# Packed scores on 64 by 32 tiles of TensorE, without the block-diagonal operand, and another order of the first element pairs

## The chip, the core and the metric

The kernel runs on one core of a Trainium2 chip. The metric is device time in microseconds (us), from launch to the last byte of the output. Engines in the text: PE is TensorE, PEld its weight loads, DVE is VectorE, ACT is ScalarE, POOL is GpSimd, SP is SyncE, which issues nearly all the DMAs here.

## What is computed

Three stages, one after the other. The first is attention through 32 packed queries per head, the only one that the change touches:

```python
s = scale * matmul(p, k^T);  a = softmax(s);  p_packed = matmul(a, v)      # 32 x 576 scores for each head
s = scale * matmul(q, p_packed^T);  out = matmul(softmax(s), p_packed)     # 576 x 32 scores for each head
```

There are 4 batch elements, 8 heads, 576 positions and 64 numbers per head. The second stage is a mixture of four experts (2304 tokens, 512 to 1024 to 512), the third one a layer `g = h - tanh(h)` with 2048 hidden columns. Everything is float32.

## The kernel before

**What a packed score costs.** Two heads lie on the 128 partitions of one k tile (`kv_k[b][j]`, head r on partitions 64r to 64r+63), so four k tiles j make one batch element b. They are taken in two groups g of two tiles (four heads). `pack_mm(b, g)` (L253) computes the scores of a group: for each tile two products of 288 columns with `pbd`, an operand of 128 rows by 64 columns that holds the two heads' queries on its diagonal blocks and zeros elsewhere, so that one product over 128 rows gives both heads' scores apart. `pbd` is made from the loaded queries `pst` by `proto` (L1062): a DVE copy for the upper and an ACT copy for the lower half, in three pieces (four tiles at the start, the tokens `D04` and `D48` for the rest), after two memsets on POOL. float32 products appear in the trace as two records each.

**What follows a group.** `pack_max` (DVE: a maximum over 576 columns, L267, and a scaling, L269), `pack_exp` (ACT, L276, with the row sums), `pack_norm` (DVE, L284 to L287), `pack_T` (PE transposes L301 and L302, ACT copies L306 and L307), `pack_pv` (PE products with v, L319, copies L326 on ACT and L327 on DVE into `ppbd`). Then for each pair of token tiles `q_mm` and `q_max` (L341, L354), `q_exp` (L365 DVE, L368 ACT), `q_sum` and `q_mul` (L374 to L383 on DVE), `q_T` (PE L398, ACT L401, DVE L402, into `a2h` and `a2l`). The scores of a group live in a PSUM tile of the pool `ps2`, which has two buffers; the products `wps` of `pack_w1` (L584) and the projections `hps` of `up` (L634) use the same two.

**What sets the order.** Strings of tokens written by hand. `START_A`, `START_L`, `START_B` cover the first 75 us; `FIRST` and others follow. A token is a stage letter with its indices (table `STAGES`): in `M10`, M is `pack_mm`, 1 the pair of elements and 0 the group counted over the pair (M10 and M11 are the third element's two groups, M12 and M13 the fourth's). A is `pack_max`, c `pack_exp`, E both, N `pack_norm`, T `pack_T`, P `pack_pv`, Q and O `q_mm` (a whole tile pair, or half of the j), J `q_exp`, R `q_sum` with `q_mul`, X `q_T`, W `pack_w1`, u and U `up` (the second projection onto the experts' hidden columns), d, h and j `down` (L739, products of 512 columns), b `prep` (ACT copy L553 of a w2 block), B `low_w2` (its rest on DVE, L545), K, V, L loads, D `proto`. PE, DVE, ACT and SP keep the written order in `START_A` and `START_L`; PE keeps it to the end, SP in the strings after. An engine works through its own row in that order: an instruction that waits holds back all that stand behind it on its engine.

Of the kernel before, what the change touches and what calls it, by code (L numbers as in the profile page):

```python
# [9 lines left out]
F32 = mybir.dt.float32  # L10
F32R = mybir.dt.float32r
U32 = mybir.dt.uint32
ACTF = mybir.ActivationFunctionType
# [42 lines left out]
MIN_HI_SQ = (1.125 * 2.0 ** -15) ** 2  # L56

START_A = (
    "f9 f1 M00 E00 M01 E01 N00 N01 f5 T00 T01 P00 P01 D04 Q00 J00 Q01 R00 W000 f6 X00 M02 K2 b00 E02 D48 B0 N02 "
)  # L60

START_L = (
    "u000 b01 J01 T02 M03 B1 E03 n N03 d000 P02 T03 R01 M10 P03 A10 X01 c10 Q02 J02 K3 V2 V3 Q03 R02 W001 O040 O041 "
    "M11 h001 X02 j001 A11 G04 c11 J03 J04 r03 I1 U0010 t03 U0011 R04 N10 "
)

START_B = (
    "a010 a011 d002 X03 X04 M12 A12 T10 c12 N11 N12 u002 M13 A13 T11 c13 N13 P10 d003 C00 T12 P11 u003 T13 W100 P12 W101 "
    "d004 P13 "
    "L2 a110 a111 k00 k01 C01 "  # L70
)
# [48 lines left out]
def kernel(  # L120
# [13 lines left out]
    nc = tc.nc  # L134
    B, S_LEN = v.shape[0], v.shape[1]
# [5 lines left out]
    def pool(name, bufs=1, stack=None, **kw):  # L141
        return (stack or ctx).enter_context(
            tc.tile_pool(name=name, bufs=bufs, **kw, **({} if kw.get('space') == DRAM else {'reuse_waits': 'tile'}))
        )
# [9 lines left out]
    p_w1 = pool("w1", 2, pa)  # L154
    p_k4 = pool("k4", 5, pa)
    p_pp = pool("pp", 2, pa)
    pbd = p_k4.tile([128, 4 * B, 64], F32, tag="k", name="pbd")
    pps = ExitStack()
    ps2 = pool("ps2", 2, pps, space=PSUM)
    ps1 = pool("ps1", 2, pps, space=PSUM)  # L160
# [5 lines left out]
    def p1t(shape, name):  # L166
        n = (4 if warm_done else 3) if psx else 1
        turn[0] += 1
        pl = psx[0] if psx and turn[0] % n > 1 else ps1
        return pl.tile(shape, F32, tag="p1" if pl is ps1 else "x1", name=name)  # L170
    p_w2 = pool("w2", 8, pa)
    att_stack = ExitStack()
    p_att = pool("att", 8, att_stack)
# [29 lines left out]
    def att_tile(b, shape, name):  # L203
        if b < 1:
            return p_att.tile(shape, F32, tag="a", name=name)
        return u2t(shape, F32, name)

    kv_k, kv_v, qs = {}, {}, {}
# [41 lines left out]

    scs, nms = {}, {}

    def pack_mm(b, g):  # L253
        sc = scs[b, g] = ps2.tile([128, 2, 512], F32, tag="p2", name="sc")
        for jj in range(2):
            j = 2 * g + jj
            for h in range(2):
                nc.tensor.matmul(  # L258
                    out=sc[64 * jj:64 * jj + 64, h, 0:288],
                    lhsT=pbd[:, 4 * b + j, :],  # L260
                    rhs=kv_k[b][j][:, 288 * h:288 * h + 288],
                )

    def pack_max(b, g):
        sc = scs[b, g]
        mx = small.tile([128, 1], F32, tag="mx", name="mx")
        nc.vector.tensor_reduce(out=mx, in_=sc[:, :, 0:288], op=ALU.max, axis=AX.XY)  # L267
        nm = small.tile([128, 1], F32, tag="nm", name="nm")
        nc.vector.tensor_scalar(out=nm, in0=mx, scalar1=-0.125, scalar2=None, op0=ALU.mult)  # L269
        nms[b, g] = nm  # L270

    def pack_exp(b, g):
        sc, nm = scs.pop((b, g)), nms.pop((b, g))
        a1 = att_tile(b, [128, S_LEN], "a1")
        ss = small.tile([128, 1], F32, tag="ss", name="ss")
        nc.scalar.activation(  # L276
            out=a1.rearrange("p (h s) -> p h s", h=2), in_=sc[:, :, 0:288],
            func=ACTF.Exp, scale=0.125, bias=nm, accum_out=ss,
        )
        a1s[b, g] = a1, ss  # L280
# [9 lines left out]
    def pack_scores(b, g):  # L290
        pack_mm(b, g)
        pack_max(b, g)
        pack_exp(b, g)
        pack_norm(b, g)
# [15 lines left out]
    def pack_pv(b, g):  # L310
        a1t, a1e = a1ts.pop((b, g))
        bi = b % 2
        pv = p1t([128, 2, 32], "pv")
        for jj in range(2):
            j = 2 * g + jj
            for c in range(5):
                for h in range(2):
                    k0 = 64 * jj + 32 * h
                    nc.tensor.matmul(  # L319
                        out=pv[64 * h:64 * h + 64, jj, :],  # L320
                        lhsT=kv_v[b][c][:, 128 * j + 64 * h:128 * j + 64 * h + 64],
                        rhs=a1t[:, c, k0:k0 + 32] if c < 4 else a1e[:, k0:k0 + 32],
                        start=(c == 0), stop=(c == 4),
                    )
        js = slice(2 * g, 2 * g + 2)
        nc.scalar.activation(out=ppbd[b // 2][0:64, bi, js, 0:32], in_=pv[0:64], func=ACTF.Copy)  # L326
        nc.vector.tensor_copy(out=ppbd[b // 2][64:128, bi, js, 32:64], in_=pv[64:128])  # L327
# [33 lines left out]
    def q_exp(p, t0):  # L361
        n, G, sc3, mx = a2s[p, t0]
        a2 = u2t([128, 512], F32, "a2")
        a23 = a2[:, 0:n].rearrange("p (g k) -> p g k", k=32)
        nc.vector.tensor_tensor(  # L365
            out=a23, in0=sc3, in1=mx[:, 0:G].to_broadcast([128, G, 32]), op=ALU.subtract
        )
        nc.scalar.activation(out=a2[:, 0:n], in_=a2[:, 0:n], func=ACTF.Exp, scale=0.125)  # L368
        a2s[p, t0] = a2, a23, G
# [36 lines left out]
    def pp_init(p):  # L406
        ppbd[p] = p_pp.tile([128, 2, 4, 64], F32, tag="ppbd", name="ppbd")
        nc.gpsimd.memset(ppbd[p], 0.0)
# [577 lines left out]
    def late_norm():  # L986
# [3 lines left out]
    STAGES = {  # L990
        "S": lambda p, i: pack_scores(2 * p + i // 2, i % 2),
        "M": lambda p, i: pack_mm(2 * p + i // 2, i % 2),
        "E": lambda p, i: (pack_max(2 * p + i // 2, i % 2), pack_exp(2 * p + i // 2, i % 2)),
        "A": lambda p, i: pack_max(2 * p + i // 2, i % 2),
        "c": lambda p, i: pack_exp(2 * p + i // 2, i % 2),
# [3 lines left out]
        "t": lambda p, i: q_mul(p, 2 * i),  # L999
        "T": lambda p, i: pack_T(2 * p + i // 2, i % 2),  # L1000
        "P": lambda p, i: pack_pv(2 * p + i // 2, i % 2),
        "Z": pp_split,
        "I": pp_init,
# [9 lines left out]
        "a": stage,  # L1013
        "b": prep,
        "B": low_w2,
        "D": lambda a, n: proto(slice(4 + a, 4 + a + n)),
        "J": lambda p, i: q_exp(p, 2 * i),
        "k": save_w2,
        "W": pack_w1,
# [20 lines left out]
    blank = u2t([128, 128], F32, "blank")  # L1040
    nc.vector.memset(blank, 0.0)
    warm = psx[0].tile([128, 4, 128], F32, tag="x1", name="warm")
    pst = p_att.tile([128, 4 * B, 32], F32, tag="a", name="pst")
    with tc.manual_schedule(engines={mybir.EngineType.SP}):
        nc.scalar.dma_start(out=pst[:, 0:4], in_=pT[:, 0:4])
        load_k(0)
# [12 lines left out]
    for i, val in enumerate((P2, Q, -T2, 0.0)):  # L1059
        nc.vector.memset(cst[:, i:i + 1], val)  # L1060
    nc.scalar.activation(out=cst[:, 3:4], in_=cst[:, 0:1], func=ACTF.Exp)
    def proto(j):  # L1062
        nc.vector.tensor_copy(out=pbd[0:64, j, 0:32], in_=pst[0:64, j])
        nc.scalar.activation(out=pbd[64:128, j, 32:64], in_=pst[64:128, j], func=ACTF.Copy)

    nc.gpsimd.memset(pbd[:, 0:4], 0.0)
    proto(slice(0, 4))
    make_identity(nc, ident)
    nc.gpsimd.memset(pbd[:, 4:], 0.0)
    pp_init(0)  # L1070
    zero_tail()
    zero_tail()
# [270 lines left out]
```

## Time and profile before

| | us |
|---|---|
| median of 3 runs (1050.61 to 1051.05) | 1050.85 |
| the profiled execution, whole time | 1050.9 |
| its span from first to last instruction | 1049.1 |
| PE busy in the span | 1041.8 |
| DVE busy | 882.9 |
| ACT busy | 622.4 |

The profile of one execution says for each engine how long it was busy (a table by stretches of the span), lists instructions in order of time with what ended an idle stretch before them (the timeline: start, duration, engine, line, operation, output<-inputs, shapes, count, then in brackets the idle time and its releaser), and follows back the chain of work that ended last. That chain is PE for 97% of the span, so the question for every stretch is whether PE has work there and what it waits for.

### The profile page before, as it was taken

To read this page: it belongs to the slowest core of one execution; us is meant where nothing else is said; L and a number is where in the kernel's file an instruction comes from. 1 tells how busy PE (TensorE), PEld (TensorE's weight loads), DVE (VectorE), ACT (ScalarE), POOL (GpSimd) and SP (SyncE) were. 2 spreads that over 40 slices of the span, in tenths; PEclk is the share of its full clock that TensorE was granted. 3 is DMA by queue.
4 is the path that set the end of the run, shared out by engine and by line. 5 is a ranking of instruction groups with operands and counts; after the bars stand their busy time and mean duration, and the time that the engine had idled before them with its cause. 6 is when DMAs were issued, how large, how long until landed. Compare 5 with 4: busy or idle time off the path is not lost.

```text
span 1049.1 us, 16510 instructions
## 1 busy us (share of the span) xinstructions
PE 1041.8 (99%) x6345; PEld 897.1 (86%) x6345; DVE 882.9 (84%) x1356; ACT 622.4 (59%) x987; POOL 161.6 (15%) x134
## 2 busy tenths in 40 slices
PE   8999999999999999999999999999999999999998
PEld 6788888888888888888888888998999899899897
DVE  5878987988987776989897986789988899988877
ACT  4555555545454355454454444678877778777775
POOL 1000032312423102424242431000000000000000
PEclk9999999999999999999999999999999999999999
DMA  9766445544663355375446254354455453574442
GB/s 345 239 204 217 153 141 179 203 172 137 215 221 130 142 186 188 122 237 181 125 187 251 93 199 183 118 221 151 180 221 196 195 211 142 200 266 162 184 171 81
DMA packets 57727, 192.75 MB, mean 184 GB/s; under 512 B 6448, under 2 KB 9136, under 8 KB 54576
## 3 DMA queue, kind: packets, MB, share of 16 engines
q1 hardware_dynamic: 57360, 191.49, 50.9%
q8 instruction: 50, 0.82, 0.3%
q14 instruction: 29, 0.24, 0.1%
q10 hardware_dynamic: 288, 0.20, 0.1%
HBM read 144.74 MB, written 46.92 MB: 183 GB/s over the span
## 4 chain that ended last, share of the span: by engine, by line
PE 97%; DVE 0%; ACT 0%; issue 0%
PE yps L739 38%; PE ops L1162 19%; PE h3ps L933 17%; PE hpx L682 8%; PE hpz L682 6%; PE wps L584 3%; PE hps L634 2%; PE pv L319 1%; PE qsc L341 1%; PE sc L258 1%; PE xps L848 0%; PE qtp L398 0%; PE tp L301 0%; PE xps L808 0%; PE ops L1192 0%; DVE qsm L374 0%
## 5 line engine op out<-in xcount | busy, mean ns | idle before, releaser
L1162 PE MATMUL ops<-wo,gh 128*128 128x512 f32 x574 | 177.6, 390 | 0.0
L1162 PEld LDWEIGHTS ops<-wo,gh 128*128 128x128 f32 x574 | 107.1, 188 | 20.5
L752 DVE SCALAR_TENSOR_TENSOR x<-yps,pn,x 128x512 f32<-128x512 f32 x126 | 93.9, 746 | 30.6 <-PE yps L739 30.1
L739 PE MATMUL yps<-w2h,h0h 128*128 128x512 f32 x288 | 115.8, 402 | 0.0
L739 PE MATMUL yps<-w2h,h0l 128*128 128x512 f32 x288 | 113.4, 394 | 0.1
L739 PE MATMUL yps<-w2h,h1h 128*128 128x512 f32 x288 | 113.1, 393 | 0.0
L739 PE MATMUL yps<-w2l,h0h 128*128 128x512 f32 x288 | 112.9, 392 | 0.0
L1162 PE MATMUL ops<-wo,gl 128*128 128x512 f32 x287 | 112.6, 392 | 0.0
L739 PE MATMUL yps<-w2h,h1l 128*128 128x512 f32 x288 | 112.5, 391 | 0.0
L739 PE MATMUL yps<-w2l,h1h 128*128 128x512 f32 x288 | 112.1, 389 | 0.0
L933 PE MATMUL h3ps<-xh,wg 128*128 128x384 f32 x384 | 103.6, 336 | 0.0
L943 ACT ACTIVATE h<-h3ps 128x384 f32<-128x384 f32 x96 | 46.9, 490 | 70.6 <-PE h3ps L933 70.6
L455 POOL TENSOR_TENSOR fo<-fo,f 128x512 f32<-128x512 f32 x32 | 43.6, 1364 | 268.9 <-DVE f L451 183.3
L682 PE MATMUL hpx<-th,wp 128*128 128x288 f32 x336 | 80.7, 295 | 0.0
L739 PEld LDWEIGHTS yps<-w2h,h0h 128*128 128x128 f32 x288 | 54.0, 187 | 20.8 <-issue 11.3
L933 PEld LDWEIGHTS h3ps<-xh,wg 128*128 128x128 f32 x384 | 69.9, 188 | 0.7
L949 DVE TENSOR_TENSOR h<-h3ps,h 128x384 f32<-128x384 f32 x72 | 39.9, 554 | 30.6 <-PE h3ps L933 26.2
L739 PEld LDWEIGHTS yps<-w2h,h0l 128*128 128x128 f32 x288 | 54.0, 188 | 12.8 <-DVE h0l L619 0.6
L739 PEld LDWEIGHTS yps<-w2h,h1l 128*128 128x128 f32 x288 | 54.1, 188 | 12.3
L739 PEld LDWEIGHTS yps<-w2l,h1h 128*128 128x128 f32 x288 | 54.1, 188 | 12.1
L933 PE MATMUL h3ps<-xl,wg 128*128 128x384 f32 x192 | 64.3, 335 | 0.0
L739 PEld LDWEIGHTS yps<-w2h,h1h 128*128 128x128 f32 x288 | 54.1, 188 | 11.6
(192 smaller groups left out, 2587.3 us busy)
## 6 DMA issues: line engine op xcount, KB each, us to landing
wg<-wing SPq DMA_DIRECT2D x24, 1792.0 KB, 7.3
wraw<-in_w_dram SPq DMA_DIRECT2D x48, 512.0 KB, 6.3
wo<-wout SPq DMA_DIRECT2D x48, 512.0 KB, 8.8
w2s<-w2h SPq DMA_DIRECT2D x16, 512.0 KB, 4.1
w2s<-w2l SPq DMA_DIRECT2D x16, 512.0 KB, 3.8
f<-in_win_dram SPq DMA_DIRECT2D x16, 512.0 KB, 5.6
f<-in_wout_dram SPq DMA_DIRECT2D x16, 512.0 KB, 4.3
wing<-f SPq DMA_DIRECT2D x32, 256.0 KB, 3.7
```

Source lines behind the costliest of these rows:

```text
L258: nc.tensor.matmul(out=sc[64 * jj:64 * jj + 64, h, 0:288], lhsT=pbd[:, 4 * b + j, :], rhs=kv_k[b][j][:, 288 * h:288 * h + 288],)
L319: nc.tensor.matmul(out=pv[64 * h:64 * h + 64, jj, :], lhsT=kv_v[b][c][:, 128 * j + 64 * h:128 * j + 64 * h + 64], rhs=a1t[:, c, k0:k0 + 32 ...
L455: nc.gpsimd.tensor_tensor(out=lf, in0=lf, in1=st[:, :, 1].bitcast(F32), op=ALU.mult)
L584: nc.tensor.matmul(out=ps[32 * j:32 * j + 32, r, :], lhsT=ppbd[p][d, bi, j, 32 * r:32 * r + 32], rhs=raw[0, c, j // 2][d, j % 2, :],)
L634: nc.tensor.matmul(out=ps[:, ff, 0:n], lhsT=a[c, p, bi][:, g, c0:c0 + 128], rhs=x[p][:, g, t0:t0 + n], start=(k == 0), stop=(k == 5),)
L682: nc.tensor.matmul(out=ps[:, ff, 0:HB], lhsT=W[a][:, slot, c0], rhs=x[b], start=(start and k == 0), stop=(stop and k == 2), skip_group_che ...
L739: nc.tensor.matmul(out=ps, lhsT=a[:, ff, o:o + 128], rhs=w[c, fp][:, ff], start=(k == 0), stop=(k == 11),)
L752: last[0] = nc.vector.scalar_tensor_tensor(out=x2[tt], in0=ps, scalar=pn[:, tt, e:e + 1], in1=x2[tt], op0=ALU.mult, op1=ALU.add,).ins
L933: nc.tensor.matmul(out=ps, lhsT=wg[n][:, a, slot, 128 * kk:128 * kk + 128], rhs=x[c][b][kk] if isinstance(x[c][b], list) else x[c][b][:, k ...
L943: nc.scalar.activation(out=hs[n][a][b], in_=xz[n]["XZ".index(i)], func=ACTF.Copy)
L949: nc.vector.tensor_tensor(out=t, in0=xz[n]["XZ".index(i)], in1=t, op=ALU.add)
L1162: nc.tensor.matmul(out=ps, lhsT=a, rhs=wo[n][ff][:, w], start=(i == 0 and ff == 0 and k == 0), stop=(i == NG - 1 and ff == 1 and k == 2), ...
```

## The change

Three things change.

The scores no longer use `pbd`. A product takes 64 partitions of k (one head) and 32 columns of queries straight from `pst`, and writes 32 partitions of the score tile; `place` gives the partitions. There are twice as many products, each on a quarter of the array of 128 by 128. `pbd`, its memsets and `proto` with its tokens go.

`pack_mm` can take both groups of an element in one run (token `m`), alternating between the groups, with the places in the second group exchanged so that eight products in a row stand on eight different tiles. It is used for the third element (`m2`) and the fourth (`m3`).

The order strings change. `b00` comes after `E02`. The third element's two groups move from `M10` (ahead of `P03`) and `M11` (after `O041`) to `m2` after `R02`, with `X01` ahead of `P03`; its maxima and exponentials stand there together. `W001` moves from ahead of `O040` to the end of `START_L`. `m3` takes the place of `M12` and `M13` and stands where M12 stood.

```diff
 START_A = (
-    "f9 f1 M00 E00 M01 E01 N00 N01 f5 T00 T01 P00 P01 D04 Q00 J00 Q01 R00 W000 f6 X00 M02 K2 b00 E02 D48 B0 N02 "
+    "f9 f1 M00 E00 M01 E01 N00 N01 f5 T00 T01 P00 P01 Q00 J00 Q01 R00 W000 f6 X00 M02 K2 E02 b00 B0 N02 "
 )
 START_L = (
-    "u000 b01 J01 T02 M03 B1 E03 n N03 d000 P02 T03 R01 M10 P03 A10 X01 c10 Q02 J02 K3 V2 V3 Q03 R02 W001 O040 O041 "
-    "M11 h001 X02 j001 A11 G04 c11 J03 J04 r03 I1 U0010 t03 U0011 R04 N10 "
+    "u000 b01 J01 T02 M03 B1 E03 n N03 d000 P02 T03 R01 X01 P03 Q02 J02 K3 V2 V3 Q03 R02 m2 A10 c10 A11 c11 "
+    "O040 O041 h001 X02 j001 G04 J03 J04 r03 I1 U0010 t03 U0011 R04 N10 W001 "
 )
 START_B = (
-    "a010 a011 d002 X03 X04 M12 A12 T10 c12 N11 N12 u002 M13 A13 T11 c13 N13 P10 d003 C00 T12 P11 u003 T13 W100 P12 W101 "
+    "a010 a011 d002 X03 X04 m3 A12 c12 A13 T10 N11 c13 N12 d003 T11 N13 P10 C00 P11 u002 T12 u003 T13 W100 P12 W101 "
     "d004 P13 "
 ...
-    def pack_mm(b, g):
-        sc = scs[b, g] = ps2.tile([128, 2, 512], F32, tag="p2", name="sc")
-        for jj in range(2):
-            j = 2 * g + jj
-            for h in range(2):
-                nc.tensor.matmul(
-                    out=sc[64 * jj:64 * jj + 64, h, 0:288],
-                    lhsT=pbd[:, 4 * b + j, :],
-                    rhs=kv_k[b][j][:, 288 * h:288 * h + 288],
-                )
+    def place(b, g, jj, r):
+        return 64 * jj + 32 * (r ^ (g if b > 1 else 0))
+
+    def pack_mm(b, *gs):
+        for g in gs:
+            scs[b, g] = ps2.tile([128, 2, 512], F32, tag="p2", name="sc")
+        for h in range(2):
+            for jj in range(2):
+                for r in range(2):
+                    for g in gs:
+                        j, d = 2 * g + jj, slice(64 * r, 64 * r + 64)
+                        k0 = place(b, g, jj, r)
+                        nc.tensor.matmul(
+                            out=scs[b, g][k0:k0 + 32, h, 0:288],
+                            lhsT=pst[d, 4 * b + j, :],
+                            rhs=kv_k[b][j][d, 288 * h:288 * h + 288],
+                        )
 ...
-                    k0 = 64 * jj + 32 * h
+                    k0 = place(b, g, jj, h)
 ...
+        "m": lambda b: pack_mm(b, 0, 1),
 ...
-    def proto(j):
-        nc.vector.tensor_copy(out=pbd[0:64, j, 0:32], in_=pst[0:64, j])
-        nc.scalar.activation(out=pbd[64:128, j, 32:64], in_=pst[64:128, j], func=ACTF.Copy)
-
-    nc.gpsimd.memset(pbd[:, 0:4], 0.0)
-    proto(slice(0, 4))
     make_identity(nc, ident)
-    nc.gpsimd.memset(pbd[:, 4:], 0.0)
```

The lines of the functions named above stand seven higher in the changed kernel (L267 becomes L274). SP's row is the same in both.

On ACT, from the split of the first pair's scores (`a2h`) on, before:

```order
L401 ACTIVATE a2h_214<-qtp_399 128x2x256
L553 ACTIVATE w2h_419<-wraw_173 128x1024
L276 ACTIVATE a1_427,ss_428<-sc_406,nm_425 128x576
L1064 ACTIVATE pbd_81<-pst_137 64x8x32
L618 ACTIVATE h0h_444<-hps_448 128x2x256
```

and in the changed kernel:

```order
L408 ACTIVATE a2h_209<-qtp_400 128x2x256
L283 ACTIVATE a1_428,ss_429<-sc_407,nm_426 128x576
L560 ACTIVATE w2h_431<-wraw_172 128x1024
L625 ACTIVATE h0h_447<-hps_451 128x2x256
L625 ACTIVATE h1h_449<-hps_466 128x2x256
```

The copy of the w2 block (`w2h`) now stands behind the exponential of M02's scores. On DVE the order at this place is as before (maximum, scaling, `w2l` of B0, then the norm N02 of the same scores), less the copy into `pbd`.

On PE, from the transposes of T03 on to the first products of h001, before (P03 is the four rows `pv`, Q02 and Q03 are `qsc` x32, W001 is `wps`, O040 and O041 are `qsc` x8):

```order
L301 MATMUL tp<-ident,a_507 128x128 x4
L302 MATMUL te<-ident,a_507 64x128
L258 MATMUL sc<-kt,pbd 64x288 x4
L319 MATMUL pv<-a1t,vt 64x32 x8
L319 MATMUL pv<-a1e,vt 64x32 x2
L319 MATMUL pv<-a1t,vt 64x32 x8
L319 MATMUL pv<-a1e,vt 64x32 x2
L398 MATMUL qtp<-ident,a_482 128x128 x4
L341 MATMUL qsc<-ppbd,qt 64x2x32 x32
L584 MATMUL wps<-wraw,ppbd 32x512 x8
L341 MATMUL qsc<-ppbd,qt 64x2x32 x8
L258 MATMUL sc<-kt,pbd 64x288 x4
```

and in the changed kernel:

```order
L308 MATMUL tp<-ident,a_514 128x128 x4
L309 MATMUL te<-ident,a_514 64x128
L405 MATMUL qtp<-ident,a_485 128x128 x4
L326 MATMUL pv<-a1t,vt 64x32 x8
L326 MATMUL pv<-a1e,vt 64x32 x2
L326 MATMUL pv<-a1t,vt 64x32 x8
L326 MATMUL pv<-a1e,vt 64x32 x2
L348 MATMUL qsc<-ppbd,qt 64x2x32 x32
L265 MATMUL sc<-kt,pst 32x288 x16
L348 MATMUL qsc<-ppbd,qt 64x2x32 x8
```

X01 (`qtp`) moved from behind M10 and P03 to directly behind T03; both groups of scores stand in one run; W001 has left this place.

On DVE, from the row sums of R02 on, before:

```order
L374 TENSOR_REDUCE qsm_679<-a2_635 128x16
L375 TENSOR_SCALAR qsm_679<-qsm_679 128x16
L378 RECIPROCAL qsm_679<-qsm_679 128x16
L383 TENSOR_TENSOR a2_635<-a2_635,qsm_679 128x512
L595 TENSOR_TENSOR wp_693<-wps_684,wp_693 128x1024
L402 TENSOR_TENSOR a2l_215<-qtp_717,a2h_214 128x2x256
L267 TENSOR_REDUCE mx_732<-sc_705 128x1
L269 TENSOR_SCALAR nm_734<-mx_732 128x1
```

and in the changed kernel:

```order
L381 TENSOR_REDUCE qsm_674<-a2_630 128x16
L382 TENSOR_SCALAR qsm_674<-qsm_674 128x16
L385 RECIPROCAL qsm_674<-qsm_674 128x16
L390 TENSOR_TENSOR a2_630<-a2_630,qsm_674 128x512
L274 TENSOR_REDUCE mx_697<-sc_679 128x1
L276 TENSOR_SCALAR nm_699<-mx_697 128x1
L274 TENSOR_REDUCE mx_704<-sc_680 128x1
L276 TENSOR_SCALAR nm_706<-mx_704 128x1
L291 TENSOR_SCALAR ss_709<-ss_709 128x1
L409 TENSOR_TENSOR a2l_210<-qtp_727,a2h_209 128x2x256
```

Both maxima of the third element, with a step that waits for an exponential, now stand ahead of X02's `a2l`; on ACT both exponentials stand ahead of its `a2h`. W001's `wp` stands behind the norms N10, further on.

## Rows read from the trace of the kernel before

**Rows 1.** Busy time by stretches: length, then each engine; PEclk, DMA share, GB/s

```profile
20.00:75.00 55.00, 54.41 (x617) 42.26 (x618) 43.52 (x98) 31.48 (x65) 1.98 (x7) 1.00 0.70 234
75.00:1045.00 970.00, 970.00 (x5496) 840.83 (x5496) 829.58 (x1232) 583.24 (x907) 155.32 (x112) 1.00 0.49 177
```

**Rows 2.** Timeline, the first scores: start, duration, instruction, idle before and releaser

```profile
1.06 4.14 PE L984 MATMUL warm<-blank 128*128 128x128 f32 x20 [1.06 <-DVE cst L1060]
...
5.48 2.21 PE L258 MATMUL sc<-kt,pbd 128*64 128x288 f32 x16 [0.28 <-ACT pbd L1064]
```

**Rows 3.** Timeline, PE at M10, W001 and M11

```profile
31.70 1.20 PE L258 MATMUL sc<-kt,pbd 128*64 128x288 f32 x8
...
36.57 1.09 PE L584 MATMUL wps<-wraw,ppbd 64*32 64x512 f32 x16
...
...
38.10 1.19 PE L258 MATMUL sc<-kt,pbd 128*64 128x288 f32 x8
```

**Rows 4.** Timeline, from M02's scores to the transposes of T02

```profile
21.56 1.06 ACT L553 ACTIVATE w2h<-wraw 128x1024 fp32r<-128x1024 f32 x1 [0.94 <-DMA wraw<-in_w_dram]
...
22.04 0.15 DVE L269 TENSOR_SCALAR nm<-mx 128x1 f32<-128x1 f32 x1
...
22.52 0.72 ACT L276 ACTIVATE a<-sc,nm 128x576 f32<-128x576 f32 x1
...
22.65 1.23 DVE L545 TENSOR_TENSOR w2l<-wraw,w2h 128x1024 fp32r<-128x1024 f32 x1 [0.26 <-ACT w2h L553]
...
23.36 0.42 ACT L1064 ACTIVATE pbd<-pst 64x256 f32<-64x256 f32 x1
...
24.18 0.52 DVE L287 TENSOR_SCALAR a<-a,rs 128x576 f32<-128x576 f32 x1
...
24.93 0.60 PE L301 MATMUL tp<-ident,a 128*128 128x128 f32 x4
```

**Rows 5.** Timeline, from T02's successors to X01 and Q02

```profile
25.76 0.69 DVE L619 SCALAR_TENSOR_TENSOR h1l<-hps,h1h 128x512 fp32r<-128x512 f32 x1 [0.46 <-ACT h1h L618]
...
31.03 0.63 PE L301 MATMUL tp<-ident,a 128*128 128x128 f32 x4
...
31.55 0.69 DVE L374 TENSOR_REDUCE qsm<-a 128x16 f32<-128x512 f32 x1
...
32.72 0.61 PE L319 MATMUL pv<-a1t,vt 128*64 128x32 f32 x16
32.77 0.69 DVE L383 TENSOR_TENSOR a<-a,qsm 128x512 f32<-128x512 f32 x1
...
33.97 0.66 PE L398 MATMUL qtp<-ident,a 128*128 128x128 f32 x4
...
34.55 2.08 PE L341 MATMUL qsc<-ppbd,qt 128*64 128x64 f32 x64
```

**Rows 6.** Timeline, from R02's product to the projection U0010

```profile
39.43 0.69 DVE L383 TENSOR_TENSOR a<-a,qsm 128x512 f32<-128x512 f32 x1
...
40.04 1.22 DVE L595 TENSOR_TENSOR wp<-wps,wp 128x1024 fp32r<-128x1024 f32 x1
...
41.34 0.60 ACT L401 ACTIVATE a2h<-qtp 128x512 fp32r<-128x512 f32 x1 [2.26 <-PE qtp L398]
...
41.97 0.69 DVE L402 TENSOR_TENSOR a2l<-qtp,a2h 128x512 fp32r<-128x512 f32 x1 [0.72 <-ACT a2h L401]
...
42.58 0.75 DVE L267 TENSOR_REDUCE mx<-sc 128x1 f32<-128x576 f32 x1
...
42.72 0.19 PEld L634 LDWEIGHTS hps<-a2l,wp 128*128 128x128 f32 x1 [0.22 <-DVE a2l L402]
```

**Rows 7.** Timeline, a wait in d002, the norms N10 and N11, M12

```profile
47.06 0.19 PEld L739 LDWEIGHTS yps<-w2h,h0l 128*128 128x128 f32 x1 [0.58 <-DVE h0l L619]
...
49.87 0.95 DVE L287 TENSOR_SCALAR a<-a,rs 128x576 f32<-128x576 f32 x2
...
50.25 1.20 PE L258 MATMUL sc<-kt,pbd 128*64 128x288 f32 x8
```

More of the change, by code (lines that the diff above doesn't have):

```diff
@@ L156 @@
     p_pp = pool("pp", 2, pa)
-    pbd = p_k4.tile([128, 4 * B, 64], F32, tag="k", name="pbd")
+    pst = p_k4.tile([128, 4 * B, 32], F32, tag="k", name="pst")
     pps = ExitStack()
@@ L1015 @@
         "B": low_w2,
-        "D": lambda a, n: proto(slice(4 + a, 4 + a + n)),
         "J": lambda p, i: q_exp(p, 2 * i),
@@ L1042 @@
     warm = psx[0].tile([128, 4, 128], F32, tag="x1", name="warm")
-    pst = p_att.tile([128, 4 * B, 32], F32, tag="a", name="pst")
     with tc.manual_schedule(engines={mybir.EngineType.SP}):
```

## The prediction

> **What bounds the kernel now.** I read the busy time by stretches first, since it says where a gain or a loss would count. From 75 to 1045 us PE is busy for all of 970 us at a granted clock of 1.00, and from 20 to 75 us for 54.41 of 55 [rows 1]. So PE is the bound behind the first 20 us, and it has no idle time in which a delay could be made good: what PE is late by at 75 us, the kernel is late by at the end. The whole change lies ahead of 75 us. I then went through the timeline of that stretch, PE's row beside the rows of DVE and ACT, and asked at each moved token two things: how much PE time it saves, and whether what PE needs next is ready in the new order.
>
> The second question matters because 54.41 of 55 us busy means that nearly every hand-off in the stretch is hidden by something, and the change moves what hides it. PE also doesn't run past a product that waits: in d002 it stood 0.58 us for `h0l` [rows 7], with the following products of the same two weights standing behind it.
>
> I write how much later (+) or earlier (-) PE comes to a place than before.
>
> **The price of the new scores.** Before, a group is four products of 288 columns on two tiles of 128 by 64, two on each; M10 starts at 31.70 and P03 behind it at 32.72 [rows 3, 5], so 1.0 us, and M11 lasts about 1.1 [rows 3]. Now a group alone is eight products on four tiles, again two on each: I take the same 1.1. The only row with tiles of 64 by 32 is W001: eight products of 512 columns on eight tiles in 1.09 us [rows 3]. A run of both groups is sixteen products of 288 columns on the same eight tiles, two on each: 2 x 1.09 x 288/512 = 1.2, less what stands in both once (the tail), so 1.1. Against 2.1 for two groups apart, `m2` and `m3` save 1.0 us of PE each. The bounds: 1.0 for a run (no fixed cost twice) and 2.2 (the two row halves not beside each other, a rival below).
>
> The rest that goes, three pieces of `proto` on DVE and ACT (0.3 to 0.42 each, as the 0.42 at 23.36 [rows 4]) and two memsets on POOL, is off PE's path except at the very start. There the first scores waited 0.28 us for ACT's copy [rows 2]; the products of the first fill end at 1.06 + 4.14 = 5.20. With the copy gone PE can start there: **-0.3**, which the chain of hand-offs behind it passes on up to M02.
>
> **T02: ACT's new order.** Before, `w2h` ran first (21.56, when its DMA had landed) and M02's exponential at 22.52, behind it [rows 4]; on DVE `w2l` ran from 22.65 while the exponential went on, and the norm followed it, ending at 24.18 + 0.52 = 24.70, just before PE came to T02 at 24.93. Now the exponential goes first: the scaling ends at 22.19, less 0.3, so it starts at 22.0 and ACT is free 0.84 later (22.52 to 23.36 in rows 4), at 22.85. `w2h` takes 1.06, to 23.9. On DVE the norm still stands behind `w2l`, and from the start of `w2l` to the norm's end it was 2.05 us (22.65 to 24.70). That gives 26.0, and T02 at 26.1: **+1.2**. PE has nothing to do there for about 1.5 us, since its projection before T02 comes 0.3 to 0.6 earlier. What is queued behind on DVE (`h0l`, `h1l`, J01, B1, the maximum of M03) moves too, but there DVE had 0.46 us of idle time [rows 5], which absorbs part: I take **+0.8** at T03, so 31.8 for 31.03.
>
> **X01: its cover is gone.** R01 begins once P02's copy is through, at 31.55 before, and its last product ended at 32.77 + 0.69 = 33.46 [rows 5]. Before, M10 and P03 (31.70 to 33.97) stood on PE between T03 and X01 and hid it. Now X01 stands directly behind T03, which ends at about 32.4, while R01 ends at 33.46 + 0.8 = 34.3: PE waits 1.9 us, X01 starts at 34.35 for 33.97, **+0.4** though M10 (1.0) and P03 (1.25) are still to come. P03 then takes 1.25 and X01 0.6: Q02 at 36.1 for 34.55, **+1.5**. Q02's second half reads what P03's copies give; X01 hid that before and now doesn't: another 0.3. Then W001 has gone (1.0) and `m2` takes the place of M11 at the same price: **+0.8** where h001 begins.
>
> **U0010: two more steps on DVE and ACT ahead of X02's split.** R02's product on DVE was at 39.43 [rows 6]; with Q02 it comes 1.4 to 1.5 later and ends at 41.6. Before, `wp` (1.22) stood next, then `a2l`, which was through when PE wanted it: PE's idle at U0010's second product was 0.22 us [rows 6]. Now two maxima with their scalings stand there (0.75 and 0.15 each [rows 4, 6]), and on ACT two exponentials of 0.84 ahead of `a2h` (0.60). The first exponential starts at 41.6 + 0.95 = 42.55, the second ends at 44.25, `a2h` at 44.9, `a2l` (0.69) at 45.55; PE goes on at 45.6 for 42.72: **+2.9**. h001, X02 and j001 cover PE up to about 43.6, so it idles near 2 us here. W001, now behind U0011, adds its 1.0 again, and the wait of d002 (0.58, some 0.4 of it lost time) falls away under it: **+3.5**.
>
> **m3: the gain and a new wait.** It saves 1.0. But it takes both buffers of `ps2` at once, and the second is W001's, free only when DVE has done `wp` (1.22 [rows 6]), which now stands behind both norms. These ended at 49.87 + 0.95 = 50.8 [rows 7]; 2.8 to 3.5 later, with 1.22 behind them, gives 54.8 to 55.5, while PE comes to `m3` at 50.25 + 3.5 = 53.75. So 1.05 to 1.75 of waiting for 1.0 saved: +0.1 as I take it. What is moved behind it (T10 to P13, d003 now ahead of T11) keeps one block of 2.7 us or more on PE ahead of each thing that it needs; I count nothing, with 0.4 either way.
>
> **Sum.** +3.6 us on PE at 75 us, and so at the end. From the profiled execution's 1050.9 (the median of the runs is 1050.85): **1054.5 us**, 0.34% slower. In other words: 2.0 of PE's time and 0.3 at the start are saved, and some 6 us of new idle time on PE stand against them, at T02 (1.5), X01 with Q02 (2.2), U0010 (2.0) and `m3` (1.1), less the 0.6 or so of waits that go.
>
> **Rivals.** *PE fills the new waits.* If PE took the products that stand behind a waiting one, as long as their own operands are there, P03 would run in X01's wait and W001 or U0011 in U0010's; the new idle time would fall from 6 us to under 1, and with 2.3 saved the kernel would end at 1049.5, faster. It decides from 3.6 us of filled time on. The weight loads do run ahead of the products, which speaks for it; the 0.58 us stood in d002 speaks against it [rows 7]. 3%.
>
> *Shorter hand-offs.* The chains at T02, X01, U0010 and `m3` hold some 25 steps between engines, of 0.03 to 0.1 us each as rows 4 to 6 show them. If the changed order lets 0.06 of each overlap, 1.5 us go: 1053.0. Only beyond that would it lie within 0.2% of before (2.1 us, about what a measurement of this kernel can tell from no change). 5% for under 2.1.
>
> *The two row halves don't run side by side.* In W001 the two row halves of the array write different PSUM banks; no row shows two of them writing one bank at the same time, in different partitions, as each group now does. If that goes one after the other, each of the four single groups takes 1.0 more on the path and each of the two runs 1.0: some 6 us, 1060.5. [...] I give it 8%, since the row that is nearest, W001's, has row halves and column strips side by side at no loss.
>
> *The clock.* [...] 4%.
>
> **How the numbers follow.** My forecast, 1054.5, has 80%. Its own range comes from the terms: hand-offs 1.5 less at most, `m3` and what follows 1.0 more, the other waits 0.3 each: 1052.9 to 1056.6, which takes in the clock's case; the bank's case and those that end within 0.2% or faster, together under 20%, are left out. Slower by over 0.2% (the forecast, the bank, the clock): 92%. Within: 5%. Faster: 3%.
>
> **What would show it.** In the changed profile: the first scores at about 5.2; ahead of T02's transposes PE idle about 1.5 us and released by DVE's norm; ahead of X01 1.9 us released by R01's product; ahead of U0010 1.3 us released by ACT's `a2h` and more by `a2l`; the runs `m2` and `m3` at 1.1 us of products, `m3` with a wait for `wp` inside; PE busy for all of the time behind 80 us. I am wrong if PE comes to the fourth element's scores (50.25 before) less than 2.1 us later, or if a single group takes 2 us.

## The result, and the profile after

The changed kernel takes 1056.70 us (median of 6 runs, 1055.68 to 1057.22) against 1050.95 (1050.61 to 1051.51): a ratio of 1.0053, 95% interval 1.0043 to 1.0064, so 0.53% slower, where 0.34% was forecast. The median lies 0.1 us above the upper end of the forecast's range. The profiled execution of the changed kernel took 1055.77 us, its span is 1053.9.

Where the time is lost shows in the same two stretches as in rows 1 (columns as there):

```profile
20.00:75.00 55.00, 50.59 (x622) 39.80 (x620) 40.00 (x88) 27.64 (x59) 2.13 (x8) 0.97 0.62 208
75.00:1045.00 970.00, 970.00 (x5533) 840.51 (x5526) 830.18 (x1234) 585.11 (x909) 155.28 (x112) 1.00 0.50 178
```

(The third number from the end is the granted clock.) Between 20 and 75 us PE is busy for 50.59 us where it was 54.41, and the mean granted clock there is 0.97 for 1.00. Behind 75 us PE has no idle time in either kernel, as forecast: from W100 on each place of PE's row stands 4.83 us later than in the first trace of before, up to the end.

The timeline of the changed kernel, PE's row at the places that the prediction speaks of:

```profile
21.00 1.18 PE L265 MATMUL sc<-kt,pst 64*32 64x288 f32 x16
27.29 0.66 PE L308 MATMUL tp<-ident,a 128*128 128x128 f32 x4 [1.34 <-DVE a L294]
33.33 0.66 PE L308 MATMUL tp<-ident,a 128*128 128x128 f32 x4
35.99 0.63 PE L405 MATMUL qtp<-ident,a 128*128 128x128 f32 x4 [1.90 <-DVE a L390]
37.78 3.57 PE L348 MATMUL qsc<-ppbd,qt 128*64 128x64 f32 x64
41.28 1.20 PE L265 MATMUL sc<-kt,pst 64*32 64x288 f32 x32
43.02 0.50 PE L746 MATMUL yps<-w2h,h0h 128*128 128x512 f32 x1
47.07 0.41 PE L641 MATMUL hps<-a2h,wp 128*128 128x320 f32 x1 [0.56 <-ACT a2h L408]
47.80 0.42 PE L641 MATMUL hps<-a2l,wp 128*128 128x320 f32 x1 [0.32 <-DVE a2l L409]
55.24 0.82 PE L405 MATMUL qtp<-ident,a 128*128 128x128 f32 x6
55.98 1.97 PE L265 MATMUL sc<-kt,pst 64*32 64x288 f32 x32
71.99 1.09 PE L591 MATMUL wps<-wraw,ppbd 64*32 64x512 f32 x16
```

These are M02, T02, T03, X01, Q02 with Q03, `m2`, h001, U0010 (two rows), X03, `m3` and W100. The waits at T02 and X01 stand in brackets with the releasers that were forecast. What was not: the 64 records of Q02 and Q03 take 3.57 us for 2.08. The granted clock of that stretch says why:

```profile
36.00:37.68 1.68, 1.68 (x43) 1.51 (x44) 0.40 (x1) 0.60 (x1) 0.00 (x0) 1.00 0.83 281
37.68:41.09 3.41, 3.41 (x70) 3.41 (x68) 1.79 (x4) 0.22 (x1) 0.99 (x2) 0.50 0.92 252
41.09:42.50 1.41, 1.41 (x42) 0.70 (x40) 1.22 (x3) 0.63 (x1) 0.00 (x0) 1.00 0.99 378
```

From 37.68 to 41.09 us the clock stood at 0.5 of its full rate; PE had idled 1.34 us ahead of T02 and 1.90 ahead of X01 before that. In all six runs the mean clock of the span is 0.998, where before has 0.999 to 1.000; a fall of 3.41 us alone takes 0.0016 off it.

### The profile page after: what moved, and what is told of

It is laid out like the page before. It is cut to its first block, busy times and chain, and to the rows that moved or that the text cites. A ratio compares the mean times of both kernels' runs of the same rounds, so it can differ in the third digit from the quotient of the medians.

```text
span 1053.9 us, 16633 instructions
## 1 busy us (share of the span) xinstructions
PE 1043.4 (99%) x6409; PEld 897.6 (85%) x6409; DVE 882.1 (84%) x1353; ACT 621.5 (59%) x984; POOL 160.4 (15%) x132
## 4 chain that ended last, share of the span: by engine, by line
PE 97%; DVE 2%; ACT 1%; issue 0%; ACTq 0%; DVEq 0%
PE yps L746 38%; PE ops L1161 19%; PE h3ps L940 17%; PE hpx L689 8%; PE hpz L689 6%; PE wps L591 3%; PE hps L641 2%; PE pv L326 1%; PE qsc L348 1%; PE warm L991 1%; PE xps L855 0%; PE sc L265 0%; PE tp L308 0%; PE qtp L405 0%; ACT a L283 0%; PE xps L815 0%
```

## The experiments

All kernels, with PE's lateness against the first trace of before, read at the same products behind 100 us and in the last ones, and the time from which the trace's record of the granted clock is full. The last three columns are of the one traced run; that of e4_b00 is its slowest, 1056.55 us:

| kernel | median us | ratio to before, 95% | PE behind 100 us | at the end | clock full from |
|---|---|---|---|---|---|
| changed kernel | 1056.70 | 1.0053 [1.0043, 1.0064] | +4.83 | +4.84 | 6.96 |
| e1_tiles | 1052.39 | 1.0015 [1.0006, 1.0024] | +1.04 | +2.17 | 6.64 |
| e2_order | 1055.32 | 1.0044 [1.0032, 1.0057] | +4.42 | +4.39 | 5.82 |
| e3_p03 | 1053.60 | 1.0025 [1.0016, 1.0035] | +1.91 | +2.67 | 5.00 |
| e4_b00 | 1053.83 | 1.0031 [1.0019, 1.0043] | +4.54 | +5.61 | 6.62 |
| e5_before | 1051.55 (one run) | | +0.67 | +0.66 | 7.13 |
| e6_both | 1052.68 | 1.0014 [1.0004, 1.0023] | +1.31 | +1.83 | 6.03 |
| e7_late | 1051.31 | 1.0002 [0.9993, 1.0012] | -0.15 | -0.14 | 4.12 |
| e8_late_m2 | 1050.70 | 0.9996 [0.9987, 1.0005] | +0.26 | +0.26 | 6.41 |
| e9_split_first | 1052.58 | 1.0016 [1.0007, 1.0025] | +1.47 | +2.13 | 5.90 |
| e10_mixed | 1049.56 | 0.9987 [0.9978, 0.9996] | -1.46 | -1.45 | 4.90 |
| e11_early | 1051.33 | 1.0004 [0.9996, 1.0013] | +1.16 | +1.18 | 7.24 |
| e12_order_of_mixed | 1051.33 | 1.0006 [0.9997, 1.0015] | +0.13 | +0.11 | 4.96 |

### The kernel before once more: its start varies

> The kernel before once more, for a second trace of its start. Theory (when the clock rises is chance in every kernel, and the products of the start take it as it comes): the granted clock rises at some other time between 4.5 and 7 us; where it rises behind 6 us, the second projection's chain (first maximum 6.74, M02 19.9) comes 0.2 to 0.7 us later than in the first trace; in the code of PE the gap of 0.23 us stands in the fill products behind W000, three records in. Rival (the tiles delay the clock): it rises at about 4.5 us again.

The clock became full at 7.13 us, for 4.54 in the first trace. First rows of before's second trace, then of the changed kernel:

```profile
5.62 2.94 PE L258 MATMUL sc<-kt,pbd 128*64 128x288 f32 x16
7.61 0.76 DVE L267 TENSOR_REDUCE mx<-sc 128x1 f32<-128x576 f32 x1 [2.39 <-PE sc L258]
```

```profile
5.62 2.78 PE L265 MATMUL sc<-kt,pst 64*32 64x288 f32 x32
7.51 0.76 DVE L274 TENSOR_REDUCE mx<-sc 128x1 f32<-128x576 f32 x1 [6.47 <-PE sc L265]
```

Before's scores take 2.94 us here for 2.21 in the first trace, the first maximum stands at 7.61 for 6.74, and 0.67 of it is still there behind 100 us. So the 0.77 us by which the changed kernel's maximum is late in its trace (7.51) need not be the change's: with the clock full at nearly the same time it is 0.1 earlier. Over all traces the clock is full at 4.12 to 7.13 us with the old scores at the start and at 5.00 to 7.24 with tiles there, seven traces each; a small part of the tiles in it is not excluded. The mean clock of a run does not show its start, since the record begins only where the clock is full. From here on the changed kernel is set against this second trace; 4.83 - 0.67 = 4.16 us is what it loses by 75 us.

Rows of that trace at M02, T02, T03, X01, Q02 with Q03, h001, U0010 (second product), X03, M12, T10, W100:

```profile
20.79 1.20 PE L258 MATMUL sc<-kt,pbd 128*64 128x288 f32 x8
25.59 0.60 PE L301 MATMUL tp<-ident,a 128*128 128x128 f32 x4
31.70 0.63 PE L301 MATMUL tp<-ident,a 128*128 128x128 f32 x4
34.63 0.66 PE L398 MATMUL qtp<-ident,a 128*128 128x128 f32 x4
35.22 2.08 PE L341 MATMUL qsc<-ppbd,qt 128*64 128x64 f32 x64
39.89 0.51 PE L739 MATMUL yps<-w2h,h0h 128*128 128x512 f32 x1
43.39 0.41 PE L634 MATMUL hps<-a2l,wp 128*128 128x320 f32 x1
50.14 0.81 PE L398 MATMUL qtp<-ident,a 128*128 128x128 f32 x6
50.89 1.20 PE L258 MATMUL sc<-kt,pbd 128*64 128x288 f32 x8
52.02 0.65 PE L301 MATMUL tp<-ident,a 128*128 128x128 f32 x4
67.83 1.09 PE L584 MATMUL wps<-wraw,ppbd 64*32 64x512 f32 x16
```

### Tiles alone, order alone

```diff
 e1_tiles: the changed kernel with the strings of before, without D04 and D48
-    R01 X01 P03 Q02 J02 ... R02 m2 A10 c10 A11 c11 ...
+    R01 M10 P03 A10 X01 c10 Q02 J02 ... M11 h001 X02 j001 A11 ...
 e2_order: the kernel before with the strings of the changed one
-    R01 M10 P03 A10 X01 ... d002 X03 X04 M12 A12 T10 ...
+    R01 X01 P03 Q02 ... R02 M10 M11 A10 c10 A11 c11 ... d002 X03 X04 M12 M13 A12 c12 A13 T10 ...
```

> The tiles of 64 by 32 alone, every group for itself, in the order of the kernel before (the block-diagonal operand and its copies gone). Theory (the loss of the changed kernel comes from its order, and the clock's late rise and its fall at 37.68 us are not the tiles' doing): the first scores start at 5.2 to 5.6, T02 and X01 without a wait of over 0.3 us, single groups at 1.2 us, granted clock 1.00 throughout from 5 us on, and the time is within 0.5 us of before (1050.4 to 1051.4). Rival (the tiles themselves make the clock rise late and the start longer, as in the changed kernel's trace, where M02 comes 1.08 us later): clock full only at about 7 us, M02 1.0 to 1.4 us late, and 1051.5 to 1052.3.

> The order of the changed kernel alone, with the block-diagonal operand of before; m2 and m3 are two groups one behind the other. Theory (order makes the loss): waits at T02 (1.3), X01 (1.9) and U0010 as in the changed kernel, the granted clock falls behind X01's wait as there, M02 at its old place (19.9), and 1054.5 to 1056.5; if the clock does not fall, 1054 to 1055. Rival (the tiles make the loss of the start, 1.1 us, and of the clock, 1.6 us): no fall of the clock, and 1052.5 to 1053.5.

T02 and X01 of e2_order:

```profile
26.42 0.66 PE L301 MATMUL tp<-ident,a 128*128 128x128 f32 x4 [1.33 <-DVE a L287]
35.16 0.63 PE L398 MATMUL qtp<-ident,a 128*128 128x128 f32 x4 [1.90 <-DVE a L383]
```

The order alone gives nearly the whole loss: T02 waits 1.33 us, X01 1.90, the clock falls at 36.54 for 3.41 us, and PE is 4.42 late. Of its five runs one, at 1055.10 us, has a mean clock of 0.999, which leaves no room for a fall of 3.41 us, and yet lost nearly as much; no trace shows how. The tiles alone have none of that (PE busy 54.57 of 55 from 20 to 75 us, clock 1.00), but cost 1.04 us behind 100 us, 0.67 of which or less is the clock's late rise, and another 1.14 at 426 us, far behind the change. So the theory on the order holds, and e1 fits neither of its two expectations in full.

### Which wait does the clock follow?

```diff
 e3_p03
-    R01 X01 P03 Q02
+    R01 P03 X01 Q02
 e4_b00
-    K2 E02 b00 B0
+    K2 b00 E02 B0
 e6_both: both edits
```

> The changed kernel with P03 put back ahead of X01, nothing else. Theory (X01's wait of 1.90 us lacks P03's 1.2 us of products as cover, and the fall of the clock at 37.68 follows from that idle time): X01's wait at 0.5 to 0.8, no second wait of over 0.4 at Q02, clock 1.00 from 8 us on, and 2.3 to 3.0 us less than the changed kernel (1053.5 to 1054.5). Rival (the fall has nothing to do with this wait): the clock falls at about 37 us for 3.4 us as before, and only 0.9 to 1.3 us come back.

> The changed kernel with b00 (w2h on ACT) put back ahead of E02, nothing else. Theory: T02's wait of 1.34 us goes down to 0.3 or less, T03 comes some 0.8 us earlier, X01's wait is then 1.6 to 1.9 and stays, and 0.6 to 0.9 us come back at the end if the clock still falls (1055.6 to 1056.2). If the fall needs both waits, it is gone too and 2.2 to 2.7 us come back.

> The changed kernel with P03 ahead of X01 and b00 ahead of E02, both. Theory (the two waits add up): T02's wait below 0.3, X01's below 0.8, clock 1.00 from the start's rise on, the wait ahead of U0010 as with P03 alone, and 0.5 to 1.3 us less than with P03 alone: 1052.3 to 1053.1. Rival (the chain on DVE and ACT ahead of U0010 sets the pace, and takes up what PE gains before it): U0010's wait grows by what T02 gives back, and the time is that of P03 alone, 1053.4 to 1053.8.

With P03 back, X01's wait is gone and one of 0.58 stands at P03; T02's 1.34 stays. In the stretch in which the changed kernel's clock had fallen this kernel shows:

```profile
37.68:41.09 3.41, 3.41 (x58) 2.08 (x54) 3.17 (x8) 0.63 (x1) 0.40 (x2) 1.00 0.93 266
```

The clock does not fall in any of its nine runs (mean clock 0.999 to 1.000). Set against the changed kernel at the same places, PE has gained 0.86 us at T02, by the start alone; from there to Q02 the cover gains 1.23, over Q02 and Q03 the clock gains 1.48, and at U0010 0.72 is lost again, where PE now waits 1.00 and 0.31 us for 0.56 and 0.32. So 2.05 of the 2.91 us that it is ahead at W100 come from the edit.

With b00 back, T02 has no wait and X01 keeps 1.74 us. The clock then falls in some runs and not in others: mean clock 0.997 at 1055.72 and 1056.55 us, 0.999 to 1.000 at 1053.17 to 1054.02 in the other four. The traced run is one that fell, for 6.83 us, and the fall begins inside X01's wait (second line: the first half of the fall, granted clock third from the end):

```profile
34.36 1.09 PE L405 MATMUL qtp<-ident,a 128*128 128x128 f32 x4 [1.74 <-DVE a L390]
33.93:37.34 3.41, 2.98 (x42) 2.68 (x42) 0.98 (x2) 0.60 (x1) 0.00 (x0) 0.50 0.69 218
```

With both back it falls in none of ten (clock 1.00 in the trace), and 0.92 us more comes back than with P03 alone: 1052.68 by the median. The idle time of 1.90 and 1.74 us ahead of X01 is thus what the fall hangs on: with 1.34 ahead of T02 it comes in six runs of six of the changed kernel, without in two of six, and 1.34 with 0.58 gives none. What decides in e4_b00 stays open.

### Why U0010 waits

```diff
 e9_split_first: e6_both, and
-    R02 m2 A10 c10 A11 c11 O040 O041 h001 X02 j001 G04
+    R02 m2 O040 O041 h001 X02 A10 c10 A11 c11 j001 G04
```

> As the kernel with both P03 and b00 back, and besides X02 with its split (a2h on ACT, a2l on DVE) ahead of the two maxima and exponentials of m2. Theory (queue: U0010 waits 1.3 us because a2h stands on ACT behind two exponentials, which wait for two maxima): a2h comes 1.3 to 1.7 us earlier, PE idles under 0.4 us ahead of U0010, and 0.9 to 1.3 us come back. Rival (buffer: m2 holds both buffers of ps2, and U0010's sums need one of them, which comes free only behind the first of those exponentials): the idle time ahead of U0010 stays at 1.2 to 2.0 us, its releaser is now the exponential of L283 and no longer a2h, and the time stays within 0.3 us of that kernel (1052.4 to 1053.0).

In e6_both PE idles 1.03 us ahead of U0010, for `a2h`, which ACT begins at 42.94 behind the exponentials, and 0.31 for `a2l`:

```profile
42.20 0.74 ACT L283 ACTIVATE a<-sc,nm 128x576 f32<-128x576 f32 x1
42.94 0.59 ACT L408 ACTIVATE a2h<-qtp 128x512 fp32r<-128x512 f32 x1
43.58 0.41 PE L641 MATMUL hps<-a2h,wp 128*128 128x320 f32 x1 [1.03 <-ACT a2h L408]
```

With the split first, `a2h` runs 1.8 us earlier, and PE waits longer:

```profile
41.15 0.60 ACT L408 ACTIVATE a2h<-qtp 128x512 fp32r<-128x512 f32 x1 [2.75 <-PE qtp L405]
43.42 0.74 ACT L283 ACTIVATE a<-sc,nm 128x576 f32<-128x576 f32 x1 [1.67 <-DVE nm L276]
44.30 0.41 PE L641 MATMUL hps<-a2h,wp 128*128 128x320 f32 x1 [1.81 <-ACT a L283]
```

The rival holds: `m2` takes both buffers of `ps2` at once, and the sums of U0010 need one of them. Whichever of the two, the split or the exponentials, comes first, PE waits for the other. The prediction had the queue right and did not see the buffer behind it; the run of two groups has this price here, where the next user of `ps2` comes soon behind it.

### Tiles for some elements only, and a version that is faster

```diff
 e7_late: the kernel before, tiles for the last two elements (single groups); pst2 holds their queries
+        if b < 2:
+            return pack_one(b, *gs)          # pack_mm of before
+                            lhsT=pst2[d, 4 * b - 8 + j, :],
 e8_late_m2: e7_late, and
-    R01 M10 P03 A10 X01 ... O041 M11 h001
+    R01 m2 P03 A10 X01 ... O041 h001
 e11_early: the reverse of e7_late
+        if b > 1:
+            return pack_one(b, *gs)
```

> The order of before; block-diagonal operand for the first two elements, tiles of 64 by 32 only for the last two (four single groups). Theory (the 1.0 us that the tiles alone cost comes from the start: eight products for four in the first two groups, and the wait inside W000 for PE's code that they shift it into): W000 without a split, M02 and T02 within 0.3 us of before in a run whose clock rises early, and 1050.7 to 1051.3. Rival (the cost comes from the single groups of the last two elements, or from the tiles' transfers): 1051.5 to 1052.5.

> As the one before, with the third element's two groups in one run at the place of the first of them (ahead of P03), nothing else moved. Theory (0.9 us of PE's time is saved, but X02 then comes before its operand is there, since the chain on DVE, Q02's maximum to the product of R02, is not shorter): X02 idle 0.5 to 0.8 us, released by DVE's product, and the time within 0.4 us of the one before. Rival (PE sets the pace there): 0.7 to 0.9 us less than the one before.

> The order of before; tiles of 64 by 32 for the first two elements alone, block-diagonal operand for the last two (the reverse of the kernel with late tiles). PE then has 16 products more ahead of the stretch at 400 us, as with the late tiles, and not 32. Theory (the tiles alone cost 1.0 us at most at the start, and the 0.5 to 1.1 us at 426 us come from where PE's code load falls, at 406 to 411 us with 32 products more): W000 split behind its third record as with all tiles, PE's code load at about 413 to 415 us, no wait of hpz at 426, and 1051.0 to 1051.5. Rival (the wait at 426 belongs to the early tiles, by their place in memory or their transfers): it is there again, and 1051.8 to 1052.6.

Late tiles cost nothing that can be measured (1051.31; PE -0.15 with an early clock). With `m2` at M10's place PE is 0.76 late at T00 and 0.26 late behind 100 us, so 0.50 is gained on the way, where e7 gains 0.03 (-0.12 and -0.15). Of the 0.9 that the run saves, X02's wait for DVE takes the rest; by the medians it is 0.61 faster than e7, between the two forecasts:

```profile
32.25 1.20 PE L277 MATMUL sc<-kt,pk 64*32 64x288 f32 x32
40.98 0.63 PE L417 MATMUL qtp<-ident,a 128*128 128x128 f32 x4 [0.41 <-DVE a L402]
```

Early tiles cost 1.16 with the clock full at 7.24, so 0.5 more than before's second trace; why is told below.

```diff
 e10_mixed: e8_late_m2, with these strings
+    u000 b01 B1 M03 T02 E03 J01 n N03 d000 P02 T03 R01 m2 A10 P03 X01 c10 Q02 J02 K3 V3 Q03 R02 W001 V2 O040 O041 h001
+    X02 j001 A11 c11 J03 G04 I1 J04 r03 U0010 t03 U0011 R04 N10
+    d002 a010 a011 X03 M12 A12 T10 X04 c12 N11 N12 u002 M13 A13 T11 c13 d003 N13 T12 C00 P10 P11 u003 T13 W100 W101
+    a110 P12 P13 d004 a111 L2 k01 C01 k00
 e12_order_of_mixed: the kernel before with these strings (M10 for m2, M11 ahead of h001)
```

> Block-diagonal operand for the first two elements (as before), tiles of 64 by 32 for the last two, the third's groups in one run at the place of the first of them, the fourth's apart; the tokens around T02 and from X04 to P13 and those of the first chunk's copies moved by one to three places. Theory (the run saves 0.9 us, of which 0.4 is kept behind X02's wait, and the moved tokens cover another 0.3 to 0.6): no fall of the clock, no W000 split, and 0.4 to 1.2 us below before, 1049.8 to 1050.6. Rival (what the run saves is taken up by the chain on DVE as a whole): within 0.3 us of before.

> The kernel before (block-diagonal operand throughout) with the order of the mixed kernel, the third element's second group at its old place ahead of h001. Theory (of the 1.3 us by which the mixed kernel is faster, the run of two groups is 0.5 and the moved tokens are 0.8): 1050.0 to 1050.4. Rival (the moved tokens bring nothing without the shorter scores): 1050.6 to 1051.1.

The mixed kernel is 0.13% faster than before (1049.56 us, ratio 0.9978 to 0.9996), a little more than forecast, and 7.1 us faster than the changed one. It keeps the block-diagonal operand where scores stand at the start, and has one run of two groups, ahead of P03. Its PE row is 0.05 early at T00 and 1.46 early from 79 us on; that of e12, which has the old scores, 0.14 and 0.96. So, by these two traces, the moved tokens are worth 0.8 and the run with its tiles 0.6. e12's expectation missed all the same: PE loses 1.04 us at 85 us, where PE waits for DVE's subtraction of the q scores:

```profile
PE qsc L338 <- DVE a L362: 1.0, 1, 1.0
```

The mixed kernel has no such wait. DVE's order there is not written by hand, and it differs: in e12 two subtractions of 0.75 us each (`tl`) and `h0l` stand ahead of this one, in the mixed kernel `h0l` alone, with the two `tl` behind it. What makes that order differ stays open.

## Why the prediction was right and where it was wrong

The sign and the mechanism were right: PE is the bound, the new order takes the cover from several waits, and nothing behind 75 us makes it good. The sum came near, 3.6 forecast for 4.16 measured, but not by its terms, so that is in part luck: the 1.3 too little at h001, where the clock fell, stands against 0.8 too much at U0010 and 1.0 behind X03. (The list in words behind the sum gives another value: its waits add to 6.8 us, and less 0.6 and the 2.3 saved that is 3.9.) Changed kernel against before's second trace:

| place on PE | forecast | measured | step, forecast | step, measured |
|---|---|---|---|---|
| M02 | -0.3 | +0.2 | -0.3 | +0.2 |
| T02 | +1.2 | +1.7 | +1.5 | +1.5 |
| T03 | +0.8 | +1.6 | -0.4 | -0.1 |
| X01 | +0.4 | +1.4 | -0.4 | -0.3 |
| Q02 | +1.5 | +2.6 | +1.1 | +1.2 |
| h001 | +0.8 | +3.1 | -0.7 | +0.6 |
| U0010, second product | +2.9 | +4.4 | +2.1 | +1.3 |
| X03 | +3.5 | +5.1 | +0.6 | +0.7 |
| W100 | +3.6 | +4.2 | +0.1 | -0.9 |

**The start** (-0.3, measured +0.2). The gain rested on fill products that end at 5.20 [rows 2]; that was one draw of the clock. In the second trace the fill runs on until the scores begin at 5.62, and no wait for `pbd` is left to save. The 0.2 is W000: the changed kernel stops inside it (below).

**T02** came as worked out: 1.34 us of idle time for 1.5, released by the norm on DVE.

**T03**: the 0.4 that DVE's idle time [rows 5] was to absorb is not there. From T02 to T03 PE itself is the bound (M03, `yps` and P02 back to back, with no idle time from 27.29 to 33.33), so its lateness passes on; slack on DVE could not help.

**X01 and Q02**: the wait of 1.90 was forecast as 1.9, and the place of P03 behind it costs 1.2 for 1.1.

**h001** (-0.7, measured +0.6) is the largest miss: the clock. The prediction gave it 4%, and the range reaches to 1056.6 for it, 2.1 us above the sum; no run shows this term. What the runs show in its place is a fall to 0.5 for 3.41 us: it comes in every run of the changed kernel, by e3 and e6 as a consequence of the wait at X01, and costs 1.49 us on Q02 and Q03 (3.57 for 2.08). The step that failed is the chance: before's rows show the clock at 1.00 without any idle time of the 1.5 and 1.9 us that were forecast, so they were no evidence that it would stay there with them.

**U0010**: 1.3 for 2.1. PE came later by the clock, so less of the chain on DVE and ACT was left to wait for (0.56 and 0.32 for some 2.0). The two misses belong together: with P03 back and no fall of the clock the wait is 1.00 and 0.31.

**m3**: +0.1 forecast, -0.9 measured. Its wait for `wp` is there, at the weight loads, 0.64 us for the 1.05 to 1.75 forecast:

```profile
56.75 0.66 PEld L265 LDWEIGHTS sc<-kt,pst 64*32 64x32 f32 x30 [0.64 <-DVE wp L602]
```

Scores and wait take 1.90 us, from 55.98 to T10 at 57.88, for two groups of 1.13 each (50.89 to 52.02 in before), so 0.36 is won. The other 0.6 comes from the tokens moved behind it, which the prediction counted at nothing; e2, with two single groups in that place, wins 0.66 from X03 to W100 by the moves.

The rest of the difference between 4.16 and the medians (1056.70 - 1050.95 = 5.75): the profiled run lies 0.93 below the median of its kernel, and before's second trace 0.60 above that of its own. The first part fits the wait at 426 us that five other kernels show and this profile does not; the untraced runs do not show what they hold.

**The bank rival** is refuted. A single group takes 1.18 us at 21.00 (M02, before 1.20), and a run of both 1.20 at 41.28: in both, two row halves of the array write one PSUM bank (the columns of one `h` in a score tile) at the same time, in different partitions, at no loss: the first four records of M02, on four tiles, start within 0.02 us of each other. (A product now takes 64 by 32, an eighth of the array and a quarter of the 128 by 64 before; the section on the change has a quarter of the array.) That rival had 1.0 us more for each. The measurement decides, for row halves that write different partitions; no kernel here has two on the same partitions of a bank. **PE fills the waits** and **shorter hand-offs** are refuted by the brackets at T02 and X01 (1.34 and 1.90 us idle, with products queued behind). The weight loads do run ahead of their products, in d002 of before by 0.23 us (47.17 for a product at 47.40).

## What to carry to other kernels

Ask of every token moved away from a wait what stood over that wait, and of every long wait that is left open (1.9 us here) whether the clock may fall behind it: here that more than doubled the price of one lost cover (1.23 us, and 1.48 for the clock). A run that shares operands or tiles saves PE's time (1.20 us here for two groups, 1.18 for one alone), but takes all its buffers at once, so look who needs one of them next. And where more, smaller instructions do the same work at the same speed, look what they move: here the stop behind the 219th record of PE's row came to stand inside W000, and they cost half a microsecond at the start, while late in a full row they cost nothing that can be measured.

## What the runs showed of the hardware

**Where PE's code loads fall.** The changed kernel stops behind the third record of W000:

```profile
16.76 1.04 PE L591 MATMUL wps<-wraw,ppbd 64*32 64x512 f32 x3
18.02 1.08 PE L591 MATMUL wps<-wraw,ppbd 64*32 64x512 f32 x13 [0.22 <-issue]
```

No semaphore releases it. All seven kernels whose first two groups are on tiles stop there, for 0.8 to 1.1 us from record to record. With the old scores W000 runs through, and the gap, where there is one (four of seven traces, 0.34 to 0.71 us), stands 16 records further on, in fill products that nobody waits for; here e7_late:

```profile
16.90 0.60 PE L1003 MATMUL warm<-blank 128*128 128x128 f32 x3
17.69 1.16 PE L1003 MATMUL warm<-blank 128*128 128x128 f32 x9 [0.19 <-issue]
```

Sixteen records are the eight products that M00 and M01 have more on tiles: in all eleven traces that have the stop it lies behind the 219th record of PE's row, whatever product stands there. In each trace an instruction transfer (queue q8) begins 0.4 to 1.0 us ahead of W000. Each moves 16,384 bytes in the traces of before and of the changed kernel. That PE stops for its code is read from this shift, since no run moved the load by itself; with tiles the transfer is through 0.3 to 0.5 us before the 219th record starts, and what PE still waits for then no trace shows.

**The same load, 400 us later.** In the six kernels that have 32 products more by then (all with early tiles but e11) such a load falls at 406 to 411 us, among a row of SP's issues, and the issues beside and behind it take long. SP's row of e1_tiles, with the transfer in the stretch from 405 to 411.5 us (queue, packets, MB, share), and the wait on PE that follows:

```profile
q8 instruction: 1, 0.02, 1.0%
406.97 1.22 SPq L542 DMA_DIRECT2D w2l<-w2s  x1
409.76 2.16 SPq L486 DMA_DIRECT2D wout<-fh  x1
426.44 0.40 PE L689 MATMUL hpz<-a2h,wp 128*128 128x288 f32 x1 [0.93 <-DVE h1l L626]
```

The same issues of e7_late, whose loads fall at 391.6 and 413.9 us:

```profile
405.80 0.42 SPq L554 DMA_DIRECT2D w2l<-w2s  x1
408.13 0.46 SPq L498 DMA_DIRECT2D wout<-fh  x1
```

What stands between is a wait on DVE ahead of `f` (L439) for ACT's `fo`, which itself waits for a load (`f<-in_win_dram`), in e1_tiles for 2.25 us. DVE's wait is 3.43 us in e1_tiles, 2.82 to 3.36 in e3, e4, e6 and e9, 1.92 in the changed kernel, 1.10 in e7_late. The longer that wait, the more PE loses at 426 us, from 0.54 for 2.82 to 1.14 for 3.43.

e11_early was the test: early tiles, but 16 products more and not 32. Its load falls at 415.3 us, `hpz` does not wait, and PE's lateness stays at 1.18 across 426 us, where e1, e3, e4, e6 and e9 lose 0.5 to 1.14. The changed kernel's profile has the slow issue (1.57 us) but no wait behind it, so the place of the load makes the loss possible, not certain.

**The clock at the start.** It became full anywhere from 4.12 to 7.24 us after the first instruction, in the same kernel at 4.54 and 7.13, and the later one ends 0.67 us later. (In the first of these traces the fill products start 0.21 us apart up to 4.42, and 0.11 apart from 4.59 on.) A profile's start is one draw of it: a step forecast from the first 10 us of one trace is no better than that.
